# Block-sparse attention and a gated MLP on one core: two of four dense attention units moved from the opening into the streamed chunks, with a third V buffer

## The chip, the core and the metric

The kernel runs on one core of a Trainium2 chip. Times are device microseconds of one execution. The engines are named as in the profile: PE (TensorE), DVE (VectorE), ACT (ScalarE), POOL (GpSimd) and SP (SyncE, which here only issues DMAs). A change of some 0.2% can be told from none when the two kernels are timed in turns.

## What is computed

Attention over 4 batches, 8 heads, 768 positions and 64 dimensions, with a mask by blocks of 32, and then a two-layer MLP on the 3072 rows that come out of it. Cut to what matters:

```python
mask = np.abs(blk_i - blk_j) <= 1
mask = mask | (blk_i == 0) | (blk_j == 0) | (blk_i == n_blocks - 1) | (blk_j == n_blocks - 1)
for qb in range(n_blocks):
    for kb in sampled_blocks[qb]:          # 3 of 24 blocks
        mask[qb*32:(qb+1)*32, kb*32:(kb+1)*32] = True
attn = softmax(np.where(mask, q @ k.T / 8, -1e9))
x = (attn @ v).transpose(0, 2, 1, 3).reshape(3072, 512)
h = x @ w_in                               # 512 x 2048
out = (h * sigmoid(1.702 * h)) @ w_out     # 2048 x 512
```

The first and the last block of 32 queries of a batch see all 768 keys; every other block sees at most eight blocks of keys.

## The kernel before

**Units, items, chunks.** A *unit* is 64 rows of x. A *dense* unit of a batch holds its first and its last block of queries against all keys; it is worked in four *items* (two halves of the heads by two halves of the keys). A *sparse* unit holds two neighbouring blocks of queries and is one item; the units of two batches that share a position form a *pair*, which shares one load of K and V. There are 4 dense units and 44 sparse ones, and eight units in the order of `self.units` form a *chunk* of 512 rows, which the MLP works on as a whole. An item has these parts: `scores` (K against Q on PE, then `least`, the maximum on DVE, L310, and `exps` on ACT, L320), `transposes` (L341, copied by ACT, L345), `values` (L375 dense, L367 sparse) with `normalise` at a unit's end, and `turn` (L430, L437, L438), which writes the unit into the chunk's x as a high and a low part.

**The order of the work** is written out by hand; each engine works its own instructions in the order in which they are issued. `first()` is the opening: it loops over the items of the first chunk and one more. A pass issues the scores of item n, the transposes of item n-1, the turn of item n-2, some conversion steps of the weights (`weights(2)`), the exponentials, the values of item n-1, and then `loads()`. Here the order is dense unit of batch 0, 1, 2, a sparse pair, dense unit of batch 3, two sparse pairs and so on, so that the first chunk holds 20 items; one item of the second chunk is done in the opening too.

After it `run()` calls `tick(m)` for m from 0 to 96. A tick does the "up" product of one tile of 128 hidden columns for one chunk (L561 to L563), the gate (L569 to L589) and the "down" product of the tile before it (L608 to L613). A chunk takes 16 ticks. `plan()` sets the attention items of the next chunk in quarters q of a tick (`QT` is 4): the scores of an item at q, together with the values of the item before it, and the transposes four quarters later (two for a dense item). `begin(q)` issues what stands at q. While the first chunk is streamed, a tick also takes conversion steps of the weights: `n0` ahead of "up", `n1` in the gate, `n2` at its end. Each weight tile (32 of them) takes four steps on DVE (L511, L513, L481 for the tile before, L522) with one absolute value (L473) and one cast (L488) on ACT, and its words are fetched two tiles ahead from ACT's queue (L463). An output weight can be converted only once the ring of three tiles has a free one.

**Loads.** K and V have rings of two buffers (`RING`). `loads()` fetches the next K when the scores of the entry two back are all issued, and the next V when the values of the entry two back are. Dense K comes in four transfers by SP, dense V in two halves, each an entry of its own. In the opening a sparse pair's K is not loaded but copied by POOL from the resident K of batches 0 and 1 (`kres`, L211 and L215); its V comes by SP (`vmid`) and by two indirect gathers from POOL (`vown`, L243). Nine tiles of the first weights (`NWIN`) have space of their own; the other seven lie in a pool that is opened when weight number 9 is due, where `kres` was.

## Time and profile before

| what | value |
|---|---|
| median of three runs | 757.74 us (757.07 to 758.30) |
| the profiled execution | 757.91 us, of which its span 756.1 us |
| PE busy | 729.4 us, 96% of the span |
| DVE busy | 400.6 us, 53% |
| ACT busy | 368.5 us, 49% |
| POOL busy | 63.3 us, 8% |
| moved by DMA | 122.88 MB, 163 GB/s over the span |
| chain that ended last | PE 77%, DVE 8%, DMA 7%, ACT 5% |

The share of busy time is an average over stages that differ, so the page alone doesn't tell what a change to one stage is worth. The opening, the first chunk of the stream and the later chunks have to be looked at one by one. The end of a matmul is modelled, so a busy PE is not always PE at its peak; the distance from one matmul's start to the next is the safer reading. The time of a chain's step is shown from the end of the step before it.

### The profile page before, as it was taken

What the parts mean: (1) busy time and instruction counts of PE and PEld (TensorE: products, weight loads), DVE (VectorE), ACT (ScalarE), POOL (GpSimd) and SP (SyncE); (2) the same over time, 40 slices, a digit from 0 to 9 for tenths busy, and PEclk for the clock granted to TensorE, in tenths of its full rate; (3) what the DMA queues carried; (4) which work ended last, traced back from release to release, by engine and by line L of the source; (5) the groups of instructions that cost most, each with busy time, mean ns of one, the idle gap of its engine ahead of it and who ended that gap; (6) DMA issues with size and microseconds to landing.
All of it is one profiled execution on the core that took longest, in us unless ns stands there. A gap on an engine that the chain in (4) does not pass through costs nothing.

```text
span 756.1 us, 18766 instructions
## 1 busy us (share of the span) xinstructions
PE 729.4 (96%) x7584; PEld 568.8 (75%) x7584; DVE 400.6 (53%) x774; ACT 368.5 (49%) x775; POOL 63.3 (8%) x103
## 2 busy tenths in 40 slices
PE   6888999999899999999999999999999999999997
PEld 3555677766688788788788788778778878888885
DVE  3789777788744544454444454444354354343333
ACT  4787656666454344454444444445444444333232
POOL 0236101010100000000000000000000000000000
PEclk9999999999999999999999999999999999999999
DMA  8899678778465354475454365354465411141111
GB/s 322 322 324 302 206 232 253 239 227 253 160 210 165 113 177 135 130 228 158 116 171 141 112 200 159 119 146 155 123 181 171 127 43 30 42 111 43 56 42 56
DMA packets 61576, 122.88 MB, mean 163 GB/s; under 512 B 7217, under 2 KB 28594, under 8 KB 61490
## 3 DMA queue, kind: packets, MB, share of 16 engines
q1 hardware_dynamic: 47922, 76.75, 33.9%
q0 software_dynamic: 6336, 23.43, 9.7%
q10 hardware_dynamic: 7232, 21.50, 8.5%
q8 instruction: 60, 0.98, 0.5%
q14 instruction: 26, 0.21, 0.1%
HBM read 111.17 MB, written 10.49 MB: 161 GB/s over the span
## 4 chain that ended last, share of the span: by engine, by line
PE 77%; DVE 8%; DMA 7%; ACT 5%; issue 2%; ACTq 1%; SPq 0%; POOLq 0%; POOL 0%; DVEq 0%
PE banks L561 11%; PE banks L613 10%; PE banks L608 10%; PE banks L612 10%; PE banks L562 10%; PE banks L563 10%; PE banks L367 5%; PE banks L291 5%; PE banks L341 4%; DMA vown<-in_v_dram,vidx 2%; DMA vown<-in_vd_dram 2%; DMA raw<-in_moe_w_out_dram 1%; DVE a L513 1%; DVE mx L310 1%; DMA raw<-in_moe_w_in_dram 1%
## 5 line engine op out<-in xcount | busy, mean ns | idle before, releaser
L561 PE MATMUL banks<-xhi,win 128*128 128x512 f32 x384 | 158.1, 412 | 2.7 <-DVE g L576 1.8
L576 DVE SCALAR_TENSOR_TENSOR g<-g,banks 128x512 f32<-128x512 f32 x83 | 57.0, 687 | 182.7 <-ACT g L569 182.7
L612 PE MATMUL banks<-wout,ghi 128*128 128x512 f32 x384 | 150.3, 391 | 0.3
L613 PE MATMUL banks<-wout,ghi 128*128 128x512 f32 x384 | 149.8, 390 | 0.7 <-DVE wout L481 0.7
L563 PE MATMUL banks<-xhi,win 128*128 128x512 f32 x384 | 150.4, 392 | 0.0
L562 PE MATMUL banks<-xlo,win 128*128 128x512 f32 x384 | 150.2, 391 | 0.0
L320 ACT ACTIVATE ex<-banks,nm 128x256 f32<-128x256 f32 (+1 forms) x208 | 87.5, 493 | 122.0 <-DVE rg L395 110.4
L569 ACT ACTIVATE g<-banks 128x512 f32<-128x512 f32 x96 | 57.7, 601 | 141.7 <-PE banks L563 141.6
L608 PE MATMUL banks<-wout,glo 128*128 128x512 f32 x384 | 106.2, 391 | 1.2 <-DVE glo L589 1.2
L550 DVE TENSOR_TENSOR wout<-wst,wout 128x512 fp32r<-128x512 f32 x80 | 55.4, 693 | 91.9 <-ACT wout L549 91.3
L581 ACT CAST ghi<-g 128x512 fp32r<-128x512 f32 x96 | 59.7, 622 | 75.7 <-DVE g L576 75.7
L561 PEld LDWEIGHTS banks<-xhi,win 128*128 128x128 f32 x384 | 72.1, 188 | 20.5 <-issue 2.0
L243 POOL DMA_INDIRECT vown<-in_v_dram,vidx x44 | 42.9, 976 | 505.6 <-PE banks L367 476.4
L612 PEld LDWEIGHTS banks<-wout,ghi 128*128 128x128 f32 x384 | 72.1, 188 | 17.5 <-ACT ghi L581 1.8
L608 PEld LDWEIGHTS banks<-wout,glo 128*128 128x128 f32 x384 | 71.8, 188 | 17.6 <-DVE glo L589 2.9
L563 PEld LDWEIGHTS banks<-xhi,win 128*128 128x128 f32 x384 | 72.1, 188 | 16.6 <-DVE win L481 0.7
L613 PEld LDWEIGHTS banks<-wout,ghi 128*128 128x128 f32 x384 | 72.1, 188 | 16.5 <-DVE wout L481 1.3
L562 PEld LDWEIGHTS banks<-xlo,win 128*128 128x128 f32 x384 | 72.3, 188 | 12.5
L310 DVE TENSOR_REDUCE mx<-banks 128x4 f32<-128x1024 f32 (+1 forms) x60 | 69.1, 1151 | 16.9 <-PE banks L302 15.4
L345 ACT COPY pt<-banks 128x512 f32<-128x512 f32 (+1 forms) x120 | 61.5, 562 | 31.5 <-PE banks L341 29.5
L341 PEld LDWEIGHTS banks<-ident,ex 128*128 128x128 f32 x448 | 51.7, 142 | 20.0 <-ACT ex L320 7.7
L589 DVE TENSOR_TENSOR glo<-g,ghi 128x512 fp32r<-128x512 f32 x96 | 65.6, 684 | 0.7 <-ACT ghi L581 0.7
(76 smaller groups left out, 730.2 us busy)
## 6 DMA issues: line engine op xcount, KB each, us to landing
wst<-ws SPq DMA_DIRECT2D x80, 256.0 KB, 2.8
kg<-in_kb_dram SPq DMA_DIRECT2D x126, 128.0 KB, 2.5
raw<-in_moe_w_in_dram ACTq DMA_DIRECT2D x16, 512.0 KB, 4.9
raw<-in_moe_w_out_dram ACTq DMA_DIRECT2D x16, 512.0 KB, 4.6
kg<-in_kb_dram SPq DMA_DIRECT2D x18, 384.0 KB, 5.1
vown<-in_vd_dram SPq DMA_DIRECT2D x8, 768.0 KB, 5.3
vmid<-in_v_dram SPq DMA_DIRECT2D x22, 260.0 KB, 5.4
qt<-in_q_dram SPq DMA_DIRECT2D x22, 256.0 KB, 4.0
```

The source lines that it names most:

```text
L310: nc.vector.tensor_reduce(out=mx.rearrange("p (i h) -> p h i", h=2), in_=self.banks[:, at:at + 2, 0:n * len(parts)].rearrange("p h (i s) - ...
L320: nc.scalar.activation(out=ex, in_=sps[h][:, n * k:n * (k + 1)], func=AF.Exp, bias=un["nm"][:, half, c:c + 1], scale=SCALE, **sums)
L341: nc.tensor.transpose(ps[:, m], g["ex"][h, i][:, k * P:(k + 1) * P], self.ident)
L345: copies.append(lambda pt=pt, ps=ps, m=m: nc.scalar.copy(out=pt[:, 0:m], in_=ps[:, 0:m]))
L561: nc.tensor.matmul(h, wih[:, k], hi[:, k], start=(k == 0), stop=False)
L562: nc.tensor.matmul(h, wih[:, k], lo[:, k], start=False, stop=False)
L563: nc.tensor.matmul(h, wil[:, k], hi[:, k], start=False, stop=(k == NCT - 1))
L581: self.nc.scalar.copy(out=ghi, in_=self.g[m][0])
L589: self.nc.vector.tensor_tensor(out=glo, in0=g, in1=ghi.bitcast(F32), op=ALU.subtract)
L608: nc.tensor.matmul(o[n], glo[:, tk[n]], woh, start=False, stop=last)
L612: nc.tensor.matmul(o[n], ghi[:, tk[n]], woh, start=(f == 0), stop=False)
L613: nc.tensor.matmul(o[n], ghi[:, tk[n]], wol, start=False, stop=False)
```

## The change

In the opening only the dense units of batches 0 and 1 are left, followed by sparse pairs; the dense units of batches 2 and 3 stand after the fifth and the eighth pair, in the second and the third chunk, so that their attention is done in the ticks of the first and the second. The first chunk then has 14 items, and the opening 15. The first eight entries of V go round three buffers instead of two, the third of which lies in the pool that the opening frees; `loads()` waits for the entry that had the same buffer. `plan()` gives a dense item four quarters and spreads the sparse ones evenly over the rest. To make room, `NWIN` goes from 9 to 7 and the scratch for the gathers' descriptors is set to 8192 bytes. A pass of the opening that follows a sparse item takes three conversion steps instead of two, and a tick in which scores start takes one step ahead of "up" instead of none. For a dense item in a tick, the work of `spread` (the factors that join the two halves of the keys) is issued with its exponentials.

```diff
-NWIN = 9
+NWIN = 7
+NV3 = 8
@@ __init__
+        self.opening = ExitStack()
+        early = self.opening.enter_context(tc.tile_pool(name="opening", bufs=1))
+        vpool = [c] * RING + [early]
+        self.vown = [p.tile([P, 2, 2 * VROW], F32, name=f"vown{i}") for i, p in enumerate(vpool)]
+        self.vmid = [p.tile([P, 2 * VROW], F32, name=f"vmid{i}") for i, p in enumerate(vpool)]
...
-        for b in range(3):
+        for b in range(2):
             dense(b)
-        sparse(0, 0)
-        dense(3)
-        for n in range(1, 2 * NU):
+        for n in range(2 * NU):
             sparse(n // NU * 2, n % NU)
+            if n in (4, 7):
+                dense(2 + n // 7)
+        for n, e in enumerate(self.vent):
+            e["at"] = n % (RING + 1) if n < NV3 else n % RING
+            e["behind"] = next((o for o in reversed(self.vent[:n]) if o["at"] == e["at"]), None)
@@ loads
-            while self.vnext < len(self.vent) and (self.vnext < RING or not self.vent[self.vnext - RING]["values"]):
-                self.load_v(self.vent[self.vnext])
+            while self.vnext < len(self.vent):
+                e = self.vent[self.vnext]
+                if e["behind"] is not None and e["behind"]["values"]:
+                    break
+                self.load_v(e)
@@ scores
         if not self.early:
-            return [lambda: (least(), exps(0)), lambda: exps(1)]
+            todo = [lambda: (least(), exps(0)), lambda: exps(1)]
+            if g["end"] and not sparse:
+                todo += [lambda part=part: self.spread(g, part) for part in range(2)]
+            return todo
@@ plan
-            room, count = end - begin - 4 * dense, len(chunks[c]) - dense
+            first = 8 if c == 1 else 0
+            room, count = end - begin - first - 4 * dense, len(chunks[c]) - dense - (c == 1)
+            spent, passed = first, 0
             for k, g in enumerate(chunks[c]):
-                q = room + 4 * (k - count)
+                if k == 0 and first:
+                    starts.append((begin, g))
+                    continue
+                starts.append((begin + spent + room * passed // count, g))
                 if self.sparse(g):
-                    q = min(8 * k, room - 6 * (count - k)) if room >= 7 * count else room * k // count
-                starts.append((begin + q, g))
+                    passed += 1
+                else:
+                    spent += 4
@@ tick
-            n0, n1, n2 = (0, 2, 4) if heavy else (2, 2, 4)
+            n0, n1, n2 = (1, 2, 4) if heavy else (2, 2, 4)
@@ first
-                weights(2)
+                weights(2 + self.sparse(before))
@@ kernel
-    nc = _bacc.Bacc("TRN2", target_bir_lowering=False, num_devices=1)
+    nc = _bacc.Bacc("TRN2", target_bir_lowering=False, num_devices=1, dynamic_dma_scratch_size=8192)
```

By `plan()` the scores of the second chunk's items then start at quarters 0, 6 and 13, those of the dense unit at 20, 24, 28 and 32 (ticks 5 to 8), and the sparse ones after it at 36, 42 and 49. In the third chunk they start at 56, 62 and 69, the dense ones at 76, 80, 84 and 88, and the rest at 92, 99, 106 and 113.

## Rows read from the trace of the kernel before

**Rows 1.** Stages: length, busy us per engine, PE clock, DMA share, GB/s

```profile
0.00:84.00 84.00, 67.39 (x1176) 43.58 (x1176) 60.46 (x150) 57.65 (x154) 28.63 (x67) 0.96 0.89 300
84.00:206.70 122.70, 117.75 (x1227) 88.22 (x1220) 97.21 (x184) 75.40 (x152) 8.43 (x8) 1.00 0.72 231
206.70:321.20 114.50, 114.50 (x1240) 91.37 (x1232) 53.51 (x100) 52.09 (x106) 7.50 (x8) 1.00 0.51 154
```

**Rows 2.** Timeline: first "up" of tick 0; two gates of the last chunk

```profile
84.01 0.50 PE L561 MATMUL banks<-xhi,win 128*128 128x512 f32 x1
...
669.23 0.60 ACT L569 ACTIVATE g<-banks 128x512 f32<-128x512 f32 x1 [1.98 <-PE banks L563]
740.11 0.60 ACT L569 ACTIVATE g<-banks 128x512 f32<-128x512 f32 x1 [2.97 <-PE banks L563]
```

**Rows 3.** Chain that ended last, ticks 3 to 5 (start, us, what); last row: timeline

```profile
109.32 0.61 DVE g L576
...
112.94 1.15 DVE mx L310
...
114.37 1.57 ACT ex L320 x4
...
118.75 0.61 DVE g L576
...
125.05 0.61 DVE g L576
...
113.10 0.39 PE L612 MATMUL banks<-wout,ghi 128*128 128x512 f32 x1
```

**Rows 4.** Timeline of PE, two dense items of the opening

```profile
32.31 0.92 PE L375 MATMUL banks<-vown,pt 128*64 128x64 f32 x24 [0.84 <-DMA vown<-in_vd_dram]
33.16 0.88 PE L302 MATMUL banks<-kg,qt 64*64 64x384 f32 x8
33.97 0.87 PE L341 MATMUL banks<-ident,ex 128*128 128x128 f32 x6
...
36.02 0.88 PE L302 MATMUL banks<-kg,qt 64*64 64x384 f32 x8
```

**Rows 5.** Timeline of PE, sparse items of the opening; fourth row: chain

```profile
45.07 1.09 PE L291 MATMUL banks<-kg,qt 64*32 64x256 f32 x32
...
48.17 1.09 PE L291 MATMUL banks<-kg,qt 64*32 64x256 f32 x32
...
52.05 0.24 PE L367 MATMUL banks<-vown,pt 128*32 128x65 f32 x1 [1.05 <-DMA vown<-in_v_dram,vidx]
...
53.05 0.81 PE banks L302 x8
...
75.25 0.68 PE L291 MATMUL banks<-kg,qt 64*32 64x256 f32 x8
```

**Rows 6.** DVE groups of the first chunk: shapes, count, busy us, mean ns

```profile
L522 DVE SCALAR_TENSOR_TENSOR a<-raw,a 128x512 int32<-128x512 int32 x26 | 17.8, 683 | 0.0
...
L511 DVE TENSOR_SCALAR a<-a 128x512 int32<-128x512 int32 x25 | 10.6, 423 | 11.8 <-ACT a L473 11.5
L310 DVE TENSOR_REDUCE mx<-banks 128x4 f32<-128x1024 f32 x8 | 9.7, 1218 | 0.2 <-PE banks L291 0.2
...
L418 DVE TENSOR_TENSOR x<-banks,rg 128x256 f32<-128x256 f32 x8 | 3.4, 424 | 0.3
```

**Rows 7.** Timeline: one DVE step without and with POOL copying

```profile
59.60 0.42 DVE L511 TENSOR_SCALAR a<-a 128x512 int32<-128x512 int32 x1
...
65.08 2.85 POOL L211 COPY kg<-kres 128x256 f32<-128x256 f32 x6
...
65.84 0.69 DVE L511 TENSOR_SCALAR a<-a 128x512 int32<-128x512 int32 x1
```

**Rows 8.** Timeline, last copy of the first pair's K; chain, a gather's landing

```profile
27.27 0.40 POOL L215 COPY kg<-kres 128x256 f32 x1 [0.30 <-issue]
...
43.68 8.33 DMA vown<-in_v_dram,vidx
```

## The prediction

> **What bounds the kernel now.** I read the stages first [rows 1]: the opening (0 to 84.0 us, attention alone) has PE busy 67.4 of 84.0 us with DVE at 60.5, ACT at 57.7 and the DMA engines at 0.89 of their time; the first chunk's MoE ticks (84.0 to 206.7) have PE at 117.8 of 122.7 and DVE at 97.2; in the second chunk PE is busy throughout and DVE for 53.5 of 114.5. So from 206.7 on only PE work counts; before that other things count too. Then the lengths: the first "up" matmul starts at 84.01 [rows 2], and the stages are cut there and where ticks 16 and 32 start theirs. The first chunk holds as much attention as the second, lacks one "down" (2.7 us by the pitch of its matmuls) and is still 8.2 us longer, so about 10.6 us of it is waiting. A tick without attention lasts 5.45 us (669.23 to 740.11 is 13 ticks), so a sparse item costs the stream (114.5 - 16 x 5.45) / 8 = 3.4 us.

> Third, the chain inside the first chunk [rows 3]. The gate product (L576) recurs after 9.43 us in a tick with scores (109.32 to 118.75) and after 6.30 in one without (118.75 to 125.05); PE needs about 7.5 and 6.8 for those two, 14.3 together. The chain runs: conversion steps and glo on DVE, then the maximum of the scores (112.94), the exponentials on ACT (114.37 to 115.94), gate and cast on ACT, two more steps, L576. DVE stands idle in the middle of it while ACT works. The first chunk is bound by this DVE/ACT chain, not by PE.

> **Part 1, the opening loses two dense units and gains one sparse pair.** It falls from 21 items to 15. A dense item in full swing takes 2.86 us (33.16 to 36.02) and there PE is nearly full: 0.85 values, 0.81 scores, 0.65 transposes and two short waits [rows 4]. The first eight items keep their order, so the ninth item's scores would stand at 33.16; but the second half of batch 1's V, which ended a wait of 0.84 us, no longer queues on SP behind the K of batch 2, because the third buffer is free at once. The copy of the probabilities ends shortly before that point, so I credit 0.5: 32.7. From the first sparse scores to the second 3.1 us (45.07 to 48.17), to the third 4.88 (to 53.05) less the 1.05 that V was late [rows 5]: the third sparse item's scores at 39.6.

> Four more loops follow, each with three conversion steps instead of two. On DVE a loop holds the maximum, 1.22 and 0.15; the normalisation, about 0.75 of which L418 is 0.42; xlo, 0.33 once overlap is taken off; and three of the four steps (0.42, 0.69, 0.68, 0.68, each some 0.08 less when they follow closely), 1.75: 4.2 us [rows 6]. PE needs 3.3 to 3.7, ACT 3.8. So DVE sets the loop. During much of it POOL copies the next pair's K, and there the same DVE step took 0.69 instead of 0.42 [rows 7]; with POOL copying for some 5 us of every two loops I add 0.4: 4.6 a loop, 18.4 for four. The tail from the last scores to the first "up" was 8.76 (75.25 to 84.01 [rows 2, 5]); 8.8 stays. 32.7 + 3.1 + 3.8 + 18.4 + 8.8 = 66.8, that is **17.2 us less**. Bounds: 4.2 a loop, 18.8 less; 5.2 a loop (the interval 48.17 to 53.05 with its wait taken out, one step of 0.6 and the lag of a full DVE put in) and one V wait of 1.3, 13.5 less.

> The cover for V: the first pair's gathers cannot start before POOL ends that pair's K copies at 27.7 [rows 8], and the landing took 8.3 us in a full stretch, so 36; the values that need it come at about 37.8. Slack is under 2 us there; for later pairs it is 6 us or more, since the third buffer lets them start a pair sooner. Bytes: 25.2 MB moved in 84 us (300 GB/s [rows 1]); two dense units take 6.3 MB out by their shapes, one pair brings 1.6 MB of V, which leaves 20.5 MB in 66.8 us, 307 GB/s. DMA stays as full as now, so it hides behind the loops, with little to spare.

> The smaller edits: the fifth pair's K is copied by POOL inside the opening (some 5 us of POOL behind the V gathers; its reader comes more than a tick later), zero, at worst 2 us. The late pool opens at weight 7 instead of 9, so that weight waits for the last reader of the resident K; this is some four ticks into the stream, long after, zero, at worst the 5 us of copying. The halved scratch for gather descriptors shows in no row; between nothing and a POOL wait of one landing, 8.3 us, of which the slack hides most; I take zero and keep 3. Dense units in the stream load K by four SP transfers and V by two instead of nine to twelve smaller ones and two gathers; nothing on SP behind them is due within three ticks.

> **Part 2, the first chunk of the stream.** It loses one sparse item and gains four dense ones and a turn. PE alone: 4 x (0.82 + 0.65 + 0.88 + 0.1) + 0.3 - 3.1 = 7.0 us more [rows 4]. By the chain: ticks with scores go from 8 to 11, seven sparse (9.4) and four dense. A dense tick saves the wider maximum, the normalisation (which lies beside the ACT wait anyway) and 0.4 of exponentials: 8.9. That is 4 x 8.9 - 9.4 - 3 x 6.3 = 7.3, and 1.5 for the dense unit's factors and three-part normalisation. Against it, the step newly put ahead of "up" in a tick with scores falls into DVE's idle stretch [rows 3] and is free there: 11 x 0.6 = 6.6, less what the ring of output weights does not let run ahead; and 0.7 more ticks' worth of work lands in ticks where PE is the longer anyway. I take **+6.5 us**, between +3 and +11.

> A wait is added here: dense transposes come two quarters after their scores, behind the same tick's "up", and PE works in order, so "down" stands behind them. In the tick shown PE is through with "up" at 113.10 while the exponentials end at 115.94 [rows 3]; in a dense tick PE would stand about 2 us. I count it as covered, because the chain makes that tick 8.9 us and PE's work in it is 7.9.

> **Part 3, the second chunk of the stream.** No conversion, DVE half idle [rows 1]: maximum and exponentials of a dense item take about 2.5 us and "up" with the values before it 3.7, so nothing waits. PE work alone, 7.0 - 0.3 + 0.2 for starts in mid-tick: **+6.9 us**, 6.5 to 8.

> **Sum.** -17.2 + 6.5 + 6.9 = -3.8 us. The profiled execution took 757.91 us (span 756.1, 1.8 around it), 0.17 over the median of 757.74: 754.1 by its own time, 753.9 beside the median.

> **Rivals.** (a) *PE's wait at the dense transposes is not covered*, and the result is slower. Price: 1.7 to 2.8 us a dense item, 7 to 11 in all, on top of PE's 7.0 with the old 10.6 of waiting staying. -17.2 + 16 + 6.9 = +5.7: 763.5. It decides from 10.3 us added in the first chunk, 0.9 uncovered per dense item. For it: the wait is certain to appear at first, and "down" stands behind it. Against: the chain, not PE, ends these ticks, and each stand of PE gives DVE time to catch up.
> [...]
> (c) *POOL's copies hold DVE up more than I count.* Rows 7 show 0.27 us for a step; if each of the three steps and the three operations of a normalisation waits for a whole copy (2.85 for six, 0.47 each) half the time, a loop takes 5.6 and the opening ends 5 us later: -12.2 + 6.5 + 6.9 = +1.2, 759. [...]
> (d) *The chance that V or the gathers' scratch binds again* (up to 4 us) is in the width of the forecast.

> **How the numbers follow.** The forecast (750.5 to 757.5) gets 0.45, (a) 0.20 (757.5 to 765), (b) 0.18 (745 to 750.5), (c) 0.17 (756 to 761). The forecast is the likeliest: 753.9. About 0.2%, 1.5 us, is what a measurement can tell here from no change. Faster by more: 0.40 of the forecast, all of (b), 0.03 of (c): 0.61. Within: 0.05 + 0.08 of (c) + 0.02 of (a): 0.15. Slower: 0.18 + 0.06: 0.24. The range 747.5 to 761.5 leaves out the lower part of (b) and half of (a), under 2 in 10; on its own side the forecast's range is 750.5 to 757.5.

> **What would show it.** First "up" at 66.8 (64 to 70.5) with no wait of PE on V after 33 us and sparse loops near 4.6; over 70, (c) or late V. Tick 0 to tick 16 at 129 us (126 to 134); over 133 with PE idle ahead of L341 in ticks 5 to 8, (a). Tick 16 to 32 at 121.4 with PE full. From tick 32 on every length as before. The whole argument falls if the loops of sparse items lower PE's granted clock, which was 0.96 over the opening [rows 1]: PE at half its speed would set the loop.

## The result and the profile after

The changed kernel takes 762.3 us against 757.2 (medians of fifteen runs each, in turns): ratio 1.0065, 95% interval 1.005 to 1.008, some 4.9 us **slower**. The prediction was 3.8 us faster, 753.9, with a range that ended at 761.5. The changed kernel's own runs lie between 758.8 and 765.8, those of before between 756.1 and 759.7.

Line numbers of the changed kernel: "up" L572 to L574, "down" L623 and L619, gate product L587, scores L299 (sparse) and L310 (dense), maximum L318, exponentials L328, transposes L352 with their copy L356, values L378 (sparse) and L386 (dense), turn L441, gather L248, POOL's copies of K L217 and L221, conversion L522, L524, L492, L533, absolute value L484.

The stages, cut where ticks 0, 16, 32 and 48 start their "up". Columns as in [rows 1]: length, busy us per engine, clock, DMA share, GB/s.

```profile
0.00:70.93 70.93, 51.95 (x1081) 33.27 (x1081) 49.67 (x122) 46.38 (x115) 34.63 (x79) 0.98 0.88 291
70.93:201.75 130.82, 122.65 (x1274) 92.83 (x1269) 103.01 (x202) 82.65 (x176) 6.83 (x6) 1.00 0.73 238
201.75:323.51 121.76, 121.76 (x1281) 95.15 (x1279) 57.23 (x109) 56.02 (x123) 7.52 (x8) 1.00 0.53 156
323.51:440.24 116.73, 114.89 (x1238) 91.29 (x1232) 52.52 (x99) 51.98 (x106) 7.51 (x8) 1.00 0.51 151
```

Against [rows 1], with each stage measured from its first "up":

| stage | before | after | difference | predicted |
|---|---|---|---|---|
| opening | 84.01 | 70.93 | -13.1 | -17.2 |
| first chunk of the stream | 122.72 | 130.82 | +8.1 | +6.5 |
| second | 114.54 | 121.76 | +7.2 | +6.9 |
| third | 114.54 | 116.73 | +2.2 | 0 |
| the rest | 320.33 | 320.72 | +0.4 | 0 |

A profile is one execution, and the openings of two executions differ by some 2 us (84.0 before, 86.1 in run 10, whose edit costs nothing that its median shows). One reason stands in the rows: in a part of the opening PE's granted clock is lower (0.50 from 26 to 29 and from 74 to 77 us before, from 26 to 28.5 us after), so that its mean over the opening is 0.96 before, 0.98 after, 0.95 in run 9, 0.94 in run 14 and 1.00 in run 4. The missing share times the length, an estimate of the most that this can cost, is 3.4 us before and 1.4 after.

Half of the 8.6 us between sum and result is in the opening. There PE's rows show stands that before did not have ([rows 4, 5] answer to them). Timeline of PE, changed kernel, in the bracket the idle time ahead and what ended it ("issue": no wait that the profile shows):

```profile
33.24 0.95 PE L386 MATMUL banks<-vown,pt 128*64 128x64 f32 x24 [1.55 <-issue]
34.12 1.09 PE L299 MATMUL banks<-kg,qt 64*32 64x256 f32 x32
...
37.20 1.09 PE L299 MATMUL banks<-kg,qt 64*32 64x256 f32 x32
...
40.07 0.44 PE L441 MATMUL banks<-ident,x 128*128 128x128 f32 x2 [0.70 <-DVE x L434]
...
42.10 1.08 PE L299 MATMUL banks<-kg,qt 64*32 64x256 f32 x28
44.11 0.62 PE L299 MATMUL banks<-kg,qt 64*32 64x256 f32 x4 [0.93 <-issue]
...
52.73 1.09 PE L299 MATMUL banks<-kg,qt 64*32 64x256 f32 x32
...
55.57 0.44 PE L441 MATMUL banks<-ident,x 128*128 128x128 f32 x2 [0.72 <-DVE x L429]
...
57.27 0.22 PE L378 MATMUL banks<-vmid,pt 128*32 128x65 f32 x1 [0.69 <-issue]
...
61.69 1.09 PE L299 MATMUL banks<-kg,qt 64*32 64x256 f32 x32
...
70.93 0.50 PE L572 MATMUL banks<-xhi,win 128*128 128x512 f32 x1
```

The scores of the ninth item stand at 34.12 (predicted 32.7), of the third sparse one at 42.10 (39.6 by the sum, 41.0 from the true start), of the last at 61.69. Two kinds of stand are in it. At 44.11 PE stops in the middle of the scores, after 28 of 32 products, with no wait that the profile shows; at 57.27 in the middle of the values. At 33.24 (where the profile names no releaser, but ACT's copy starts at 32.71), and once more at 51.42, PE waits for a copy by ACT, and ACT and DVE waited just before for PE, which had long been done. The second of these, all engines:

```profile
47.60 1.05 POOL L248 DMA_INDIRECT vown<-in_v_dram,vidx  x1 [1.96 <-PE banks L378]
48.38 1.09 PE L352 MATMUL banks<-ident,ex 128*128 128x128 f32 x8
48.95 0.94 POOL L248 DMA_INDIRECT vown<-in_v_dram,vidx  x1 [0.30 <-issue]
49.82 0.44 PE L441 MATMUL banks<-ident,x 128*128 128x128 f32 x2 [0.34 <-DVE x L429]
50.67 1.22 DVE L318 TENSOR_REDUCE mx<-banks 128x4 f32<-128x1024 f32 x1 [0.91 <-PE banks L441]
50.72 1.08 POOL L217 COPY kg<-kres 128x256 f32<-128x256 f32 x3 [0.83 <-PE banks L441]
50.78 1.07 ACT L356 COPY pt<-banks 128x512 f32<-128x512 f32 x2 [1.11 <-PE banks L441]
51.42 0.30 PE L378 MATMUL banks<-vown,pt 128*32 128x65 f32 x2 [1.17 <-ACT pt L356]
```

PE's transposes ran from 48.38 to 49.5, yet ACT's copy of them, DVE's maximum of scores that were older still, and POOL's copy all start together at 50.7. The trace also records when PE's signals to the other engines arrive: none between 47.50 and 50.59, then five within 0.22 us. They were held, while those of DVE went through (PE's turn at 49.82 follows DVE's x). The ends of matmuls are modelled, so the trace can't tell whether only the signals came late or the ends of the products too; that PE had gone on shows in the start of its turn. The hold ends 0.7 us after POOL has issued a pair's second gather (49.89). At 32.49, four signals at once, it is the same, 0.7 us after a gather that ended at 31.79.

The four stands (1.55, 0.93, 1.17, 0.69) make 4.3 us; the opening missed its sum by 4.1. That the two figures are so near is in part chance: 1.1 of the 4.1 were lost between 37.20 and 42.10, where PE waited 0.70 us for DVE's x and stood 0.25 at 41.54, and the four loops behind, which hold three of the stands, are only 1.2 over their sum. PE also waits for DVE's x in two of those loops (0.34 and 0.72).

### The profile page after: what moved, and what is told of

It is laid out like the page before. It is cut to its first block, busy times and chain, and to the rows that moved or that the text cites. A ratio compares the mean times of both kernels' runs of the same rounds, so it can differ in the third digit from the quotient of the medians.

```text
span 761.0 us, 18756 instructions
## 1 busy us (share of the span) xinstructions
PE 726.5 (95%) x7584; PEld 566.8 (74%) x7584; DVE 399.3 (52%) x774; ACT 368.4 (48%) x775; POOL 67.8 (9%) x113
## 4 chain that ended last, share of the span: by engine, by line
PE 71%; DMA 3%; DVE 3%; ACT 2%; issue 1%; SPq 1%; ACTq 0%; DVEq 0%
PE banks L572 10%; PE banks L619 10%; PE banks L574 10%; PE banks L623 10%; PE banks L573 10%; PE banks L624 9%; PE banks L378 4%; PE banks L299 4%; PE banks L352 4%; DMA raw<-in_moe_w_in_dram 2%; DMA wst<-ws 1%; PE banks L441 1%; DMA raw<-in_moe_w_out_dram 1%; DVE g L587 1%; DVE mx L318 0%
## 5 line engine op out<-in xcount | busy, mean ns | idle before, releaser
L572 PE MATMUL banks<-xhi,win 128*128 128x512 f32 x384 | 158.0, 411 | 4.5 <-ACT wst L585 3.4
L328 ACT ACTIVATE ex<-banks,nm 128x256 f32<-128x256 f32 (+1 forms) x208 | 87.5, 493 | 133.5 <-DVE rg L406 87.2
L623 PE MATMUL banks<-wout,ghi 128*128 128x512 f32 x384 | 151.3, 394 | 0.0
L574 PE MATMUL banks<-xhi,win 128*128 128x512 f32 x384 | 150.3, 391 | 0.0
L587 DVE SCALAR_TENSOR_TENSOR g<-g,banks 128x512 f32<-128x512 f32 x83 | 57.1, 688 | 175.9 <-ACT g L580 175.8
L619 PE MATMUL banks<-wout,glo 128*128 128x512 f32 x384 | 106.2, 391 | 1.9 <-DVE glo L600 1.8
L572 PEld LDWEIGHTS banks<-xhi,win 128*128 128x128 f32 x384 | 72.1, 188 | 22.5 <-ACT wst L585 4.8
L248 POOL DMA_INDIRECT vown<-in_v_dram,vidx x44 | 43.1, 980 | 505.2 <-PE banks L378 342.0
L619 PEld LDWEIGHTS banks<-wout,glo 128*128 128x128 f32 x384 | 71.8, 188 | 17.7 <-DVE glo L600 2.7
L574 PEld LDWEIGHTS banks<-xhi,win 128*128 128x128 f32 x384 | 72.1, 188 | 16.1
L623 PEld LDWEIGHTS banks<-wout,ghi 128*128 128x128 f32 x384 | 72.1, 188 | 15.3
L318 DVE TENSOR_REDUCE mx<-banks 128x4 f32<-128x1024 f32 (+1 forms) x60 | 69.1, 1151 | 22.5 <-PE banks L310 13.0
L356 ACT COPY pt<-banks 128x512 f32<-128x512 f32 (+1 forms) x120 | 61.4, 563 | 27.2 <-PE banks L352 24.0
L352 PEld LDWEIGHTS banks<-ident,ex 128*128 128x128 f32 x448 | 51.5, 141 | 19.9 <-ACT ex L328 8.5
```

The lines of the kernel that those rows point to most:

```text
L318: nc.vector.tensor_reduce(out=mx.rearrange("p (i h) -> p h i", h=2), in_=self.banks[:, at:at + 2, 0:n * len(parts)].rearrange("p h (i s) - ...
L328: nc.scalar.activation(out=ex, in_=sps[h][:, n * k:n * (k + 1)], func=AF.Exp, bias=un["nm"][:, half, c:c + 1], scale=SCALE, **sums)
L352: nc.tensor.transpose(ps[:, m], g["ex"][h, i][:, k * P:(k + 1) * P], self.ident)
L356: copies.append(lambda pt=pt, ps=ps, m=m: nc.scalar.copy(out=pt[:, 0:m], in_=ps[:, 0:m]))
L572: nc.tensor.matmul(h, wih[:, k], hi[:, k], start=(k == 0), stop=False)
L574: nc.tensor.matmul(h, wil[:, k], hi[:, k], start=False, stop=(k == NCT - 1))
```

## The experiments

Each ran in turns with the kernel before on the same chip.

**1. Order and starts in the first chunk.** Sparse items start at even quarters, so that scores never stand in mid-"up":

```diff
-                starts.append((begin + spent + room * passed // count, g))
+                starts.append((begin + spent + room * passed // count // 2 * 2, g))
```

> The changed kernel with the starts of sparse items rounded down to an even quarter, so that no scores start in the middle of an up product (13 becomes 12, 49 becomes 48, 69 becomes 68, 113 becomes 112; 99 becomes 98). Theory: in ticks 3 and 12 the exponentials go ahead of the gate on ACT, so the next tick's up waits for the copy of h, 1.53 and 1.87 us in the profile of the changed kernel; without these starts the stretch from the first up of tick 0 to that of tick 16 falls from 130.8 by 3 to 3.5 us and the whole by as much (about 759). Rival: the DVE/ACT chain sets the length of the first chunk; the waits only move to another place and the stretch stays within 1 us of 130.8.

761.98 us, ratio 1.0045 (1.0024 to 1.0066); first chunk 131.3. In the changed kernel PE waits in the first chunk for the ring of ACT's copies (L585), and at the dense transposes for the exponentials:

```profile
100.18 0.50 PE L572 MATMUL banks<-xhi,win 128*128 128x512 f32 x1 [1.53 <-ACT wst L585]
113.11 1.11 PE L352 MATMUL banks<-ident,ex 128*128 128x128 f32 x6 [1.27 <-ACT ex L328]
122.42 0.89 PE L352 MATMUL banks<-ident,ex 128*128 128x128 f32 x4 [0.60 <-ACT ex L328]
177.09 0.51 PE L572 MATMUL banks<-xhi,win 128*128 128x512 f32 x1 [1.87 <-ACT wst L585]
```

With even quarters both waits at L572 are gone, and a longer one stands at the dense transposes. Timeline of PE in this run:

```profile
118.16 1.12 PE L352 MATMUL banks<-ident,ex 128*128 128x128 f32 x4 [4.00 <-ACT ex L328]
```

Behind that wait PE's granted clock is 0.53 from 116.0 to 123.2 us, so the first chunk of this profile alone doesn't decide. The median does: 762.0 against 762.3, where the theory had 759. So the DVE/ACT chain sets this stage and the place of PE's wait does not.

**2. The step ahead of "up" taken out again.**

```diff
-            n0, n1, n2 = (1, 2, 4) if heavy else (2, 2, 4)
+            n0, n1, n2 = (0, 2, 4) if heavy else (2, 2, 4)
```

> The changed kernel with no conversion step ahead of up in ticks where scores start (as in the kernel before). Theory of the prediction: the step falls into DVE's idle stretch and is worth up to 6.6 us; without it the first chunk of the stream grows from 130.8 us by 3 to 6.6. Rival: the steps are the same work in another place, the chunk stays within 1 us, or even falls because the step ahead of up held back the product of the gate.

780.48 us, ratio 1.0289 (1.0261 to 1.0317). The first chunk takes 150.5 us, 20 more. What PE waits for most is weights, 12 us (waits in the first chunk of this run: us in total, times, longest):

```profile
PE banks L623 <- ACT wout L499: 6.7, 3, 2.8
PE banks L624 <- DVE wout L492: 3.3, 4, 1.5
PE banks L574 <- DVE win L492: 2.0, 2, 1.5
```

With 11 ticks of 6 steps and 5 of 8 there are 106 steps, hardly more than the 102 that the stage needs (four for each of 32 tiles, less 26 in the opening). The step isn't a filler for an idle stretch, it is supply.

**3. Two V buffers in use**, the room for the third still given up:

```diff
-NV3 = 8
+NV3 = 0
```

> The changed kernel with two V buffers in use instead of three (the third stays allocated). Theory A: the third buffer takes away waits for V; with two the opening (first up at 70.9 us) grows by 3 to 6 us. Theory B: the third buffer fills the DMA queues so that PE stands at places where no wait is recorded (1.55, 0.93 and 0.69 us in the opening); with two buffers these three stands vanish, waits for V return, and the opening stays within 2 us of 70.9.

759.48 us, ratio 1.0016 (0.9994 to 1.0039): faster than with three: the two intervals do not meet. In its profile the opening is 70.5, as theory B says, with a wait for V of 1.22 at 40.09, but a stand of 1.38 is left at 55.49; the first chunk is 133.3.

**4. The order of before, the rest of the change kept** (NV3 11).

> The order of units of the kernel before (four dense units in the opening) with all the rest of the changed kernel: third V buffer for the first eleven entries, seven early weight tiles, the extra steps. It takes the move of the dense units apart from the rest. If the move is what costs, this is faster than the kernel before by the three waits for V in its opening (0.84, 1.05, 1.34 us): about 754, with the stream unchanged at 122.7 and 114.5 us for its first two chunks. If the rest costs too (steps, the stands of PE), it is no faster than 757.

759.75 us, ratio 1.0022 (1.0002 to 1.0043). The V waits of [rows 4, 5] are gone and the opening is 81.9 (at a mean clock of 1.00, 0.96 before); the first chunk takes 125.5 instead of 122.7. So the rest of the change costs too.

**5. The third buffer alone:** the kernel before with the buffer and what it needs; order, starts and steps of before.

> The kernel before with the third V buffer alone (its order, its starts and its conversion steps stay; seven window tiles and the small descriptor scratch come with the buffer). In the run of the old order with the rest of the change the opening fell from 84.0 to 81.9 us and the first chunk of the stream rose from 122.7 to 125.5. Theory A, the buffer only takes away the waits on V, and the 2.8 us in the first chunk came from the steps and the odd starts: opening 81.5 to 82.3, first chunk 122.5 to 123, 1.5 to 2.2 us faster than before (ratio 0.997 to 0.998). Theory B, the buffer's side effects (seven instead of nine window tiles, small scratch) cost the first chunk something: first chunk 124 to 125.5, ratio 0.999 to 1.001.

760.74 us, ratio 1.0032 (1.0011 to 1.0052), so the buffer by itself is a loss. First chunk 125.9. Timeline of this run in tick 3, the first and the last of POOL's four gathers and ACT's wait for weights:

```profile
95.30 0.96 POOL L248 DMA_INDIRECT vown<-in_v_dram,vidx  x1 [23.00 <-PE banks L378]
99.05 0.94 POOL L248 DMA_INDIRECT vown<-in_v_dram,vidx  x1 [0.30 <-issue]
105.75 0.66 ACT L484 ACTIVATE a<-raw 128x512 f32<-128x512 f32 x1 [3.50 <-DMA raw<-in_moe_w_out_dram]
```

and of the kernel before, the first of two gathers:

```profile
96.19 0.94 POOL L243 DMA_INDIRECT vown<-in_v_dram,vidx  x1 [13.93 <-PE banks L367]
104.27 0.66 ACT L473 ACTIVATE a<-raw 128x512 f32<-128x512 f32 x1 [1.14 <-DMA raw<-in_moe_w_out_dram]
```

Where the third buffer is given up, two pairs' V come due at once: four gathers in a row instead of two, and the weights behind them land later.

**6. One unit moved instead of two:** three dense units in the opening, NV3 9, the fourth after the fifth pair.

> The changed kernel with three dense units in the opening and only the fourth moved, into the second chunk's attention; the attention of the first chunk of the stream is then four dense and six sparse items as in the changed kernel, the third chunk has none. Theory A, a moved unit costs the stream what it saves the opening: the opening is 6.5 us shorter than with four units (81.9 less 6.5, 75.4 us), the first chunk of the stream 130.8 as in the changed kernel, the second 114.5: 757 to 758.5, ratio 0.999 to 1.001. Theory B, the long run of sparse items in the opening is what spoils the change (PE stands there with no wait recorded): with five sparse items behind the dense ones instead of seven the stands of PE without a recorded wait shrink below 0.5 us in sum, and the opening ends at 73 to 74.5, ratio 0.996 to 0.998. If the stands stay as large as in the changed kernel (2.5 us or more), the opening ends at 77 or later and the ratio is 1.001 to 1.004.

765.18 us, ratio 1.0086 (1.0056 to 1.0117), against all theories: the opening is 84.1 instead of 75.4. Its trace has the longest hold of all, behind four gathers:

```profile
73.17 0.44 PE L441 MATMUL banks<-ident,x 128*128 128x128 f32 x2 [0.35 <-DVE x L429]
73.54 0.94 POOL L248 DMA_INDIRECT vown<-in_v_dram,vidx  x1 [0.30 <-issue]
74.78 0.93 POOL L248 DMA_INDIRECT vown<-in_v_dram,vidx  x1 [0.30 <-issue]
76.71 1.22 DVE L318 TENSOR_REDUCE mx<-banks 128x4 f32<-128x1024 f32 x1 [3.60 <-remote]
76.83 1.08 ACT L356 COPY pt<-banks 128x512 f32<-128x512 f32 x2 [3.81 <-remote]
77.47 0.32 PE L378 MATMUL banks<-vown,pt 128*32 128x65 f32 x1 [3.86 <-ACT pt L356]
```

PE's transposes were done at 72.8; the gathers end at 75.7; all engines go on at 76.7. With a second hold at 51.1 to 54.4 and other waits that are not all accounted for here, the price of one moved unit can't be read from this run.

**7. Two conversion steps in each pass** of the opening:

```diff
-                weights(2 + self.sparse(before))
+                weights(2)
```

> The changed kernel with two conversion steps in each pass of the opening, also behind a sparse item, instead of three. Theory A, DVE sets the loop of a sparse item: each of some six passes is 0.4 to 0.6 us shorter, the first up product starts at 67 to 68.5 instead of 70.9, and the first chunk of the stream takes the steps over and is 3 us longer (133 to 134.5): ratio 1.005 to 1.008, no gain. Theory B, PE's stands and POOL's copies set the loop: the opening ends at 69.5 to 71 as in the changed kernel, the first chunk is 2 to 4 us longer, ratio 1.008 to 1.012.

762.69 us, ratio 1.0059 (1.0033 to 1.0085). The four loops after the third sparse scores took 5.5, 5.3, 5.2 and 4.3 us, no less than with three steps (5.3, 5.4, 5.2, 3.7). The opening is 69.3, 1.6 shorter, but ahead of the sparse items (1.0) and behind the last scores (1.3), not in the loops; the first chunk took 134.4, at a mean clock of 0.97. The ratio lies in the range given for theory A, the loops speak against it: DVE's steps do not set them.

**8 and 12. PE's instructions counted off against the work.** Small products without a use ahead of the first turn (64, then 32):

```diff
+        if un["n"] == 0:
+            for i in range(32):
+                nc.tensor.matmul(xt[0:BLK, 0:DV], self.ident[:, 0:BLK], self.ident[:, 0:DV], ...)
```

> The changed kernel with 64 small extra matrix products (128 instructions of PE with their weight loads) ahead of the first turn in the opening, whose results nobody reads; they add some 2 to 3 us there. They only shift the count of PE's instructions by 128 against the work. Theory A, PE stands because its next instructions have not been fetched: the stands without a recorded wait stay at the 962nd, 1473rd and 2255th instruction of PE, which are now 128 instructions earlier in the work (about three fifths of a sparse item's 212). Theory B, something in the work itself holds PE (a buffer, a semaphore that the trace does not show): the stands stay at the same item and operation and their count rises to 1090, 1601 and 2383.

Each product turned out to be four instructions, so that the count moved by 256 and the run (767.1 us, once) could not decide.

> The changed kernel with 32 small extra products, 128 instructions of PE, ahead of the first turn; with 64 products the count had grown by 256, a whole number of the 256 instructions between two stands, which could not tell the theories apart. Theory A, PE stands where its next block of instructions has not been fetched: stands in the middle of an operation stay at the old counts (962, 1473, 1729), now 128 instructions earlier in the work. Theory B, something at one place of the work holds PE: the counts become 1090, 1601 and 1857. The stand in the first ticks, at the count 2255, waits for POOL's copies or for instructions: 2383 by the first, 2255 by the second.

762.17 us, once. Timeline of PE in the run with 32:

```profile
42.49 0.22 PE L378 MATMUL banks<-vmid,pt 128*32 128x65 f32 x1 [1.07 <-issue]
48.38 0.24 PE L378 MATMUL banks<-vmid,pt 128*32 128x65 f32 x1 [1.55 <-issue]
58.73 0.62 PE L299 MATMUL banks<-kg,qt 64*32 64x256 f32 x4 [1.18 <-issue]
78.95 0.59 PE L299 MATMUL banks<-kg,qt 64*32 64x256 f32 x2 [0.53 <-issue]
```

Counting weight loads and products in the order of the trace, these stand at 961, 1218 and 1729, all on the old grid of 256 instructions (962, 1473 and 1729 in the runs without them), and so in other operations than in the changed kernel: the 962nd was in the third item's scores there and is in the values before it here. The trace shows 16 KB packets of an instruction queue 2.4 to 2.8 us before PE goes on (39.70, 45.88 and 56.32 here, 41.47 for 44.11 in the changed kernel). So these stands keep to the count of PE's instructions and not to the work, as theory A says; that PE waits there for its next instructions is inferred from the counts and the packets. The stand in tick 1 moved with the work (2255 to 2383), which speaks against that cause; what makes it stays open, 0.5 to 1.4 us.

**9. The order alone:** the changed kernel with two V buffers, nine window tiles, whole scratch.

> The changed kernel without the third V buffer and without what was given up for it: two V buffers, nine window tiles, the whole scratch for the gathers; order, starts and steps as changed. The run with two buffers in use but the room still given up took 759.5 us. Theory A, the buffer and its room are what costs, and the moved units are an even trade: 756.5 to 758.5, ratio 0.999 to 1.001, opening at 70 to 71.5, first chunk of the stream 129 to 131. Theory B, the order costs by itself, and the room given up costs nothing: 759 to 760.5, ratio 1.001 to 1.004, as with two buffers in use.

760.04 us, ratio 1.0018 (0.9995 to 1.0041). Opening 71.6, first chunk 131.0, second 121.8: the two moved units take 12.4 us from the opening and give 15.5 to the stream. The median is where theory B has it; the interval takes in theory A and no change as well. It does not meet that of the changed kernel (1.005 to 1.008).

**10. The room alone:** the kernel before with seven window tiles and the small scratch.

> The kernel before with only the room given up: seven window tiles instead of nine and a scratch of 8192 bytes for the gathers, two V buffers, order and steps of before. The prediction counted this at zero. If it is free: ratio 0.9985 to 1.0015, opening 84, first chunk 122.7. If it is what cost 3 us in the first chunk when the third buffer stood alone (125.9 instead of 122.7): ratio 1.003 to 1.005 with a first chunk of 125 to 126.

758.78 us, ratio 1.0008 (0.9988 to 1.0029), first chunk 123.1: no cost that can be told from none. The opening of its profile is 86.1, with the longer waits for V (1.70 at 32.59, 2.14 at 53.42), at the mean clock of before (0.96).

**11. V one pass later** than the third buffer allows:

```diff
+                if self.early and e["u"] is not None and self.passed < 2 * n_pair(e) + 5:
+                    break
```

> The changed kernel with the V of each sparse pair of the opening fetched one pass later than the third buffer lets it start, one pass earlier than two buffers would. Theory A, the third buffer sends two pairs' V into the stretch in which the DMA engines are full (10 to 40 us), so that the weights land late and ACT's queue stands 2.6 to 3.4 us for them at 28 to 31 us: the wait shrinks to below 1.5 us, and the time is 759 to 761, ratio 1.002 to 1.005, nearer to the run with two buffers in use (759.5) than to the changed kernel (762.3). Theory B, when V starts makes no difference: 761.5 to 763, ratio 1.005 to 1.008.

760.04 us, ratio 1.0037 (1.0012 to 1.0063), and its profile has an opening of 69.3 without a hold. ACT's wait for weights, 2.6 us at 28.05 in the changed kernel, is gone. All this is as theory A has it; the upper end of the interval still reaches into theory B.

**13. No weights in the opening**, order and buffers as in 9.

> The new order with two V buffers and nothing given up for a third, but with no conversion steps behind the fifth pass of the opening, so that hardly any weights are fetched there and DVE and ACT have only the attention; the first chunk of the stream will be some 20 us longer for want of weights, as without the step ahead of up, and only the opening is looked at. Theory A, the opening's loops are set by DVE, ACT and DMA together with the weights: sparse loops fall from 4.9 to 3.9 us or less, the opening ends at 63 to 66 us instead of 71.6, and PE's stands at the 962nd, 1473rd and 1729th instruction shrink below 0.4 us each, since the DMA engines have room. Theory B, PE's rate of instructions in a row of sparse items is what holds the loops: the stands stay at 0.9 us or more each and the opening ends at 67 to 70.

795.0 us, once. The loops after the first sparse one were 5.0, 3.7, 5.3, 4.2 and 5.2 us, 23.4 in all, against 5.6, 4.4, 4.2, 6.1 and 5.0, 25.2 in all, in run 9. Run 9 from 35 to 60 us and in its last loop, and then this run from 35 to 60 us (columns as above):

```profile
35.00:60.00 25.00, 20.43 (x498) 13.62 (x491) 22.44 (x49) 18.20 (x43) 18.92 (x36) 0.94 0.85 273
57.40:62.40 5.00, 4.87 (x109) 3.15 (x107) 3.36 (x8) 2.80 (x8) 4.27 (x9) 0.72 0.96 246
```

```profile
35.00:60.00 25.00, 20.79 (x552) 14.91 (x552) 15.13 (x38) 15.98 (x41) 17.18 (x39) 1.00 0.64 196
```

DVE went from 22.4 to 15.1 busy us of 25 and the DMA engines from 0.85 to 0.64, and the loops got 0.4 us shorter, to 4.7, where theory A had 3.9 or less. Even the 0.4 is not shown to be DVE's, since run 9 has a wait for V of 1.1 in its loops (41.86) and a granted clock of 0.72 in the last of them. In each of the three long ones five signals of PE came at once (42.53, 51.52, 60.91), 0.6 to 0.7 us after a second gather. The stands at the grid shrank below 0.3 us. The first "up" at 74.8 says nothing, since it waits for weights.

**14. The third buffer alone, given up two entries sooner** (NV3 9).

> The kernel before with the third V buffer alone, as in the run that took 760.7 us, but with the third buffer given up two entries sooner (after nine instead of eleven), so that the V of two pairs isn't fetched at one go at 94 to 99 us in the stream. Theory A, the 3 us that the buffer cost in the first chunk came from these four gathers in a row, ahead of which the weights land late: first chunk 122.5 to 123.5, opening 82 to 83.5, ratio 0.997 to 1.000. Theory B, the room given up or chance sets it: first chunk 125 or more, ratio 1.002 to 1.004.

758.18 us, ratio 1.0007 (0.9988 to 1.0026); first chunk 122.8, as in the kernel before. So the four gathers in a row were the 3 us of run 5. The opening of the profiled execution (89.7, at a mean clock of 0.94; it was the longest of the run's twelve) can't be used. With the old order, what the buffer brings is then nothing that can be told from none.

**15 and 16. The gathers taken off POOL**, their bytes kept (the rows are fixed ones, so the sparse items' V is not the right one):

```diff
-            nc.gpsimd.indirect_dma_start(
-                out=self.vown[r][:, j], out_offset=None, ...)
+            nc.sync.dma_start(out=self.vown[r][:, j], in_=v[BLK * j:BLK * j + P])
```

> The changed kernel with the two gathers of each sparse V replaced by two plain transfers of the same size from SP (fixed rows instead of the rows that the sampled blocks name, so that the V of the sparse items is not the right one); POOL then issues no gathers and the bytes stay. In the changed kernel's trace PE's signals to the other engines were held twice and came in a burst, at 32.49 (four) and 50.59 us (five), each 0.7 us after the end of a gather's issue on POOL. Theory A, the gathers' issue holds them: no burst of four or more, no stand of all engines there, the opening ends 1.5 to 3 us sooner (68 to 69.5), while the stands at the 962nd and 1473rd instruction of PE stay. Theory B, the hold has another cause (full DMA engines, PE's own fetches): bursts at other places, opening 70 to 72.

765.2 us, once. No hold is left, but the opening is 75.8: the plain transfers stand on SP's queue ahead of the next Q.

```profile
46.89 0.68 PE L297 MATMUL banks<-kg,qt 64*32 64x256 f32 x8 [5.61 <-DMA qt<-in_q_dram]
```

Less that wait it would be 70.2, not the 68 to 69.5 expected; the price in the changed kernel is not shown by it.

> The new order with two V buffers, no conversion steps behind the fifth pass of the opening, and the two gathers of each sparse V replaced by two plain transfers of the same size from SP (fixed rows, so that the V of the sparse items is not the right one). With the gathers the sparse loops alternated between 3.7 to 4.2 and 5.2 us, and a burst of five held signals of PE stood in each of three long ones (42.53, 51.52, 60.91 us), 0.65 us after a gather's issue ended. Theory A, the gathers' issue holds PE's signals: no such bursts, and all loops are 3.5 to 4.2 us. Theory B, the pair's other work on POOL, the copies of K, or late V makes the second loop long: loops of 5 us or more remain.

795.6 us, once. PE's scores in this run, and its two stands:

```profile
35.66 0.66 PE L297 MATMUL banks<-kg,qt 64*32 64x256 f32 x16
39.38 1.08 PE L297 MATMUL banks<-kg,qt 64*32 64x256 f32 x28
42.20 0.62 PE L297 MATMUL banks<-kg,qt 64*32 64x256 f32 x4 [1.74 <-issue]
45.44 0.88 PE L297 MATMUL banks<-kg,qt 64*32 64x256 f32 x24
49.16 0.66 PE L297 MATMUL banks<-kg,qt 64*32 64x256 f32 x16
54.25 0.22 PE L376 MATMUL banks<-vmid,pt 128*32 128x65 f32 x1 [1.77 <-issue]
54.94 0.88 PE L297 MATMUL banks<-kg,qt 64*32 64x256 f32 x24
58.66 1.09 PE L297 MATMUL banks<-kg,qt 64*32 64x256 f32 x32
```

The loops are 3.7, 6.1, 3.7, 5.8 and 3.7; without the two stands at the grid 3.7, 4.3, 3.7, 4.0, 3.7. So in this pair of runs, one execution each, the holds went with the gathers, as theory A says: with them the long loops had 5.0 to 5.3, some 1.2 us more. (Eleven of the sixteen profiles with gathers have no burst of four signals either.) But loops of over 5 us remain, as theory B says, though for another reason: from the first sparse scores to the last it is 26.1 us here and 26.4 in run 13, since the stands at the grid, below 0.3 us there, are 1.7 us each now. The DMA share is the same in both (0.62 and 0.64 from 35 to 60 us), so full DMA engines are not what makes these stands come and go; that PE, no longer held, reaches its next instructions before they are there is the author's inference, which no run shows.

## Why the prediction was wrong

**The step that failed is "DVE sets the loop", 4.2 us plus 0.4, and with it the opening's -17.2.** Runs 7 and 13 took a third of DVE's steps, then all of them, out of the loops. The first left the loops as long, the second left 4.7 us a loop. What the changed kernel's profile shows in its place are terms that the sum put at nothing: in the 19.6 us of its four loops PE stood for 3.9, of them 1.17 behind a hold of its signals, 0.93 and 0.69 at the grid of 256 instructions, and 0.34 and 0.72 for DVE's x at the turn. What is taken from one of these came back at another: with fewer steps (run 7) the hold was 1.63 and the stands 1.20 and 0.99, and without holds (run 16) the stands were 1.74 and 1.77. The figure 4.6 was near the measured 4.9 for the wrong reason. From the first sparse scores to the last the sum had 25.3 us (3.1, 3.8 and 18.4); the changed kernel took 27.6, and with neither steps nor gathers it is still 26.1. By the sum's own terms: the ninth item 1.4 late (the hold at 32.5), the third sparse item 1.1 (0.70 for DVE's x, 0.25 a stand), the four loops 19.6 instead of 18.4, the tail 9.2 instead of 8.8.

Run 9 warns against calling the holds the cause of the whole: its profile has none, and yet its ninth item stands at 34.11 and its four loops take 19.6, by other waits (2.03 for DVE's x at 25.68, 1.18 at the grid, at 56.44) and a lower clock in the last loop. So it is shown that DVE's steps do not set the loop, and which waits fill it in each execution; what makes their sum come out alike stays open. The point at which the forecast saw its argument fall, PE's clock in the sparse loops, was not it in the changed kernel, where the clock is 1.00 from 35 to 60 us; in the last loop of run 9 it was 0.72.

**V's cover.** PE has no recorded wait for V behind 33 us, as forecast; with that, 3.2 us of waits in the opening of before (0.84 and 1.05 in [rows 4, 5], and 1.34 at 73.6) are gone, while those for dense V ahead of that point went from 1.2 to 2.2. The opening is not shorter for it: 70.9 with the buffer, 71.6 in run 9 without, which has no hold of four signals and one wait for V of 1.1. By runs 9, 5 and 14 the buffer gains nothing with either order.

**The second step that failed is that earlier transfers hide behind the loops, at no cost.** With the new order the buffer costs more than the move: the ratio is 1.0065 (1.005 to 1.008) with it, and 1.0016 and 1.0018 without (runs 3 and 9; neither interval reaches 1.005). So by the ratios some 3.6 of the 4.9 us go with the buffer and some 1.3 with the order, the latter not clear of no change. As in run 5, POOL issues two pairs' gathers in a row, here from 28.18 to 33.69 us, and run 11, which parts them, comes out between. From 25 to 35 us the DMA engines' share is 1.03 in the changed kernel and 0.68 in run 9, and DVE is busy for 4.6 us instead of 7.5. Which stage then pays for it is not shown: the two profiled executions are only 1.3 us apart.

**The first chunk, +8.1 for +6.5.** The chain's part (7.3 + 1.5 = 8.8) was about right: the four dense ticks (5 to 8) took 36.0 us, 9.0 each for the 8.9 counted. The credit for the step ahead of "up" was mis-sized in kind: it was called free relief, and run 2 shows that it is needed for weights; of the 2.3 us that the forecast took off the chain's 8.8, at most 0.7 came. (The 10.6 us of waiting in this stage are 10.9 by the forecast's own terms, 8.2 and 2.7; no sum hangs on the 0.3.) **The second chunk** came as worked out (7.2 for 6.9).

**The small edits.** The room was rightly put at nothing (run 10). What was left out is the point at which the third buffer is given up: in the old order it costs 3 us (runs 5 and 14).

**The third chunk's 2.2 us** are one late transfer of an output weight (ACT's cast at 349.05 had waited 6.15 us for it); all the other profiles have 114.5 to 114.6 there, so this is taken for no part of the change. The profiled execution is near the median with it, so executions without it must lose some 2 us elsewhere, which no profile shows.

**The rivals.** (a) PE's wait at the dense transposes appeared as said, at 1.27 and 0.60 us, and no cost of its own was found (run 1); the time came out near its 763.5 by another road. (c) named POOL and gave 759, near in size, but by its copies of K; the holds in the traces stand behind its gathers. That a step of DVE waits for a whole copy is not shown by any run; taking DVE's steps out from beside the copies (run 13) freed at most 0.4 us a loop. (b), at 745 to 750.5, had it the wrong way. (d) PE did not wait for V again behind 33 us; the buffer cost in another way.

**What was behind the sign.** The move is a trade: PE's work leaves the opening and comes back in the stream, 12.4 to 13.1 us against 15.3 to 15.5. A gain could come from waits alone. Even with the sparse run of 26.1 us (run 16) in place of 27.6 the sum would be -14.6 and +15.3, about even.

## What to carry to other kernels

Moving work from a stage with slack to one that PE fills pays no more than the waits that it removes (here 12.4 to 13.1 us went out and 15.3 to 15.5 came back), so list those waits first and ask what runs in their place. Before a loop is costed by its busiest engine, take that engine's work out of one run: if the loop hardly moves, the sum is right only by chance. Compare the stages of two profiles only with their granted clocks beside them (means of 0.94 to 1.00 over the openings here), and a cost of 2 us by medians. A buffer that lets transfers start sooner also moves them beside other work (here four gathers in a row, and a first chunk of 125.9 us in run 5 against 122.8 in run 14); where a ring changes length, look for transfers that come due together.
